# A new hand-written order of calls for the opening of a fused linear-attention and MLP kernel

## The chip, the cores and the metric

The kernel runs on one core of a Trainium2 chip. Its time is the device time of one execution in microseconds (us); several executions of the same program are timed, and their median counts. Beside them one execution is taken by the hardware profiler; it has a time of its own and a span, from its first instruction to its last. The engines are TensorE (PE in the profile, its weight loads PEld), VectorE (DVE), ScalarE (ACT), GpSimd (POOL) and SyncE (SP, which here only issues transfers).

## What is computed

Linear attention with a decay per head, in blocks, and behind it a two-layer MLP whose activation has a slope `alpha` for negative values. q, k and v are (4 batches, 8 heads, 768 positions, 64), the weights 512 x 2048 and 2048 x 512, all float32.

```python
for b in range(nb):                      # blocks of 64 positions
    intra = einsum('bhic,bhjc->bhij', qb, kb) * Dmask
    intra = einsum('bhij,bhjd->bhid', intra, vb)
    inter = einsum('bhid,bhde->bhie', qb * lam_pow, kv_state)
    out[:, :, sl] = intra + inter
    kv_state = lam_block * kv_state + einsum('bhsd,bhse->bhde', kb * rev_pow, vb)
x = out.transpose(0, 2, 1, 3).reshape(3072, 512)
h = x @ w_in
return (maximum(h, 0) + alpha * minimum(h, 0)) @ w_out
```

## The kernel before

The work is cut into six chunks (L41) of 512 tokens: chunk c holds 256 positions (block pair c // 2) of two batches (2 * (c % 2) and the next one, `bi` 0 and 1). Attention goes by units: unit n is a chunk, a `bi` and a half of the heads (`hh`), n = 4c + 2bi + hh (L240), so that chunk 0 is units 0 to 3 and chunk 1 units 4 to 7. The blocks used are of 128 positions, two in a unit.

What a unit needs, by the names in the code: `load` (L80) brings k, q or v of one chunk and `bi` as float32 through SP's queue, for all heads (`None`, 512 KB) or one half of them (256 KB). `cast` (L257) makes a half-precision copy of q, k or v of a unit on ScalarE ("A"), VectorE ("V") or GpSimd ("G"). `key_decayed` (L270) multiplies the raw k by its decay. `transposed` (L313) transposes q (x = 0) or k (x = 1) of a unit on TensorE, four products into a PSUM bank ("op", "tk" or "h"), and copies them out; `transposes` (L287) does both at once, or by a transfer ("D", from unit 9 on). `decayed` (L331) multiplies the transposed q by its decay, out of SBUF or, with "P", out of PSUM on VectorE. `cluster(old, new)` (L346) then does the products: for the unit `old` the part from the state (RD) and the part from masked scores and v, for the unit `new` its scores and the state's update; then VectorE's two mask products (L416), the copy of the result of `old` into XT (L423) and the states: for the first block pair two RD copies and an R copy on ScalarE (L436, L437) and two R updates on VectorE (L440), later R updates and four copies on GpSimd (L454). The accumulator `acc` (L350) has one buffer, so one cluster's products wait until the copies of the one before have read it.

The MLP of a chunk: `up(c, f)` (L459) is one of 16 groups of columns of w_in, four products over 512 tokens or, with `bi`, over 256; ScalarE takes relu(-h) (L472), VectorE makes g (L481). `down(c, t, part, 4)` (L488) is a quarter of the sum for 128 output rows. The weights come in quarters, cast on the way, by GpSimd's queue (`load_win`, `load_wout`); up(c, f) needs quarter f // 4 of w_in, and part p of a down-product quarter p of w_out. `gate` (L109) puts a tiny transfer that reads a weight quarter into SP's queue, so that all loads behind it wait until that quarter is there.

The decay tables are made by ScalarE and VectorE in the opening: `mask_logs` (L193) on VectorE, which reads `rel_f` in the bank "op"; `decay_mask`, `key_decay`, `state_decay` and `query_decay` (L206 to L229) on ScalarE. `fill(n)` (L133) issues n products of 128x512 whose result nothing reads ("unread" in the profile).

The schedule is by hand (L30): every engine and queue takes its instructions in the order in which the calls stand, and waits where its data or its buffer isn't ready. From L565 to L866 this order is a flat list of calls, the opening: the set-up, all of chunk 0 and 1, and the start of chunk 2; behind it a loop (L868) weaves the rest by a fixed pattern. In the list before, unit 0 to 3's clusters stand at L608, L618, L625, L634, L637 and L643, the unread products at L571, L575, L609, L623 and L627, the first up-product at L641, the first down-product at L677. SP's loads of chunk 0 start with both halves of k of `bi` 0, then q, then v; the two gates are at L633 and L670.

Of the kernel before, what the change touches and what calls it, by code (L numbers as in the profile page):

```python
# [11 lines left out]
def kernel(  # L12
# [24 lines left out]
    B, H, S, D = q.shape  # L37
# [418 lines left out]
    G = {}  # L456
# [105 lines left out]
                a[i]()  # L562
                i += 1

    query_decay(2, 0)  # L565
    query_decay(2, 1)
    load(0, 0, "k", 1)
    load(0, 0, "k", 0)
    load(0, 0, "q", None)
    query_decay(1, 1)  # L570
    fill(11, "h")  # L571
    load(0, 0, "v", 0)
    mask_logs(0)
    mask_logs(2)
    fill(6, "h")  # L575
    load(0, 0, "v", 1)
    key_decay()
    key_decayed(0, "G")
    mask_logs(3)
    load(0, 1, "k", 0)  # L580
    cast(1, "k16", "G")
    cast(0, "v16", "G")
    decay_mask(0)
    cast(0, "k16", "V")
    mask_logs(1)
    cast(2, "k16", "G")
    key_decayed(1, "G")
    load_win(0)
    load(0, 1, "q", None)
    cast(0, "q16", "V")  # L590
    state_decay()
    transposed(0, 1, "V", "op")
    load(0, 1, "k", 1)
    decay_mask(2)
    transposed(0, 0, "V", "h")
    transposed(1, 1, "V", "op")
    query_decay(0, 1)
    load(0, 1, "v", None)
    decay_mask(1)
    key_decayed(2, "G")  # L600
    load(1, 0, "k", 0)
    decay_mask(3)
    load_win(1)
    query_decay(3, 1)
    decayed(0, "P")
    cast(1, "q16", "A")
    load_win(2)
    cluster(None, 0)  # L608
    fill(5, "h")  # L609
    transposed(1, 0, "A", "h")  # L610
    cast(1, "v16", "A")
    cast(3, "q16", "G")
    transposed(2, 1, "V", "h")
    decayed(1, "P")
    load_win(3)
    cast(2, "q16", "V")
    load_wout(2)
    cluster(0, 1, "A")  # L618
    transposed(2, 0, "A", "tk")
    cast(2, "v16", "V")  # L620
    decayed(2, "V")
    cast(4, "k16", "V")
    fill(8, "h")  # L623
    load(1, 0, "q", 0)
    cluster(1, 2, "A")  # L625
    cast(3, "k16", "A")
    fill(5, "op")  # L627
    cast(3, "v16", "G")
    cast(4, "q16", "G")
    transposed(3, 0, "V", "tk")  # L630
    key_decayed(3, "V")
    transposed(3, 1, "A", "h")
    gate(2, "out")  # L633
    cluster(2, None, "A")  # L634
    load(1, 1, "k", 1)
    key_decayed(4, "G")
    cluster(None, 3, "A")  # L637
    decayed(3, "G")
    slopes()
    transposes(4, "A", False)  # L640
    up(0, 1, 0, "h")  # L641
    up(0, 3, 0, "op")
    cluster(3, None, "A")  # L643
    up(0, 2, 0, "h")
    load(1, 0, "v", 0)
    up(0, 2, 1, "h")
    decayed(4, "V")
    load(1, 0, "q", 1)
    load_wout(0)
    up(0, 0, None, "op")  # L650
    up(0, 7, None, "tk")
    up(0, 5, None, "h")
    load_wout(1)
    up(0, 6, None, "op")
    up(0, 10, None, "tk")
    up(0, 11, None, "h")
    zero_states((2,), "G")
    up(0, 14, None, "h")
    load(1, 0, "k", 1)
    load(1, 1, "q", 1)  # L660
    query_decay(3, 0)
    up(0, 13, None, "tk")
    up(0, 15, None, "op")
    up(0, 4, 1, "h")
    up(0, 4, 0, "h")
    load(1, 0, "v", 1)
    load(1, 1, "v", 1)
    up(0, 9, None, "tk")
    load(1, 1, "q", 0)
    gate(1, "out")  # L670
    up(0, 12, None, "op")
    up(0, 3, 1, "h")
    up(0, 8, None, "h")
    query_decay(0, 0)
    up(0, 1, 1, "tk")
    load(1, 1, "k", 0)
    down(0, 0, 0, 4, "op")  # L677
    down(0, 2, 0, 4, "h")
    down(0, 2, 1, 4, "h")
    key_decayed(7, "G")  # L680
    load_wout(3)
    load(1, 1, "v", 0)
    zero_states((3,), "V")
    load(2, 0, "k", 0)
    cast(4, "v16", "G")
    key_decayed(5, "G")
    cast(7, "q16", "A")
    load(2, 0, "q", 0)
    down(0, 3, 0, 4, "h")
    cast(6, "k16", "G")  # L690
    cast(5, "q16", "V")
    cast(5, "k16", "V")
    down(0, 3, 1, 4, "h")
    cluster(None, 4)
    transposes(5, "A", False)
    load(2, 0, "v", 0)
    cast(6, "v16", "G")
    load(2, 0, "q", 1)
    cast(5, "v16", "A")
    cast(7, "v16", "V")  # L700
    down(0, 0, 1, 4, "op")
    decayed(5, "V")
    load(2, 1, "k", 0)
    cast(7, "k16", "A")
    cast(8, "q16", "G")
    down(0, 2, 2, 4, "h")
    query_decay(1, 0)
    load(2, 0, "k", 1)
    cluster(4, 5, "A")
    transposes(7, "A", False)  # L710
    load(3, 1, "q", 0)
    key_decayed(8, "G")
    decayed(7, "P")
    down(0, 0, 2, 4, "op")
    cast(6, "q16", "A")
    down(0, 3, 2, 4, "h")
    cluster(5, 7, "A")
    down(0, 0, 3, 4, "op")
    cast(10, "k16", "G")
    load(2, 1, "k", 1)  # L720
    load(2, 1, "q", None)
    load(2, 0, "v", 1)
    key_decayed(6, "V")
    transposes(6, "A", False)
    load(3, 0, "v", None)
    down(0, 2, 3, 4, "h")
    load(2, 1, "v", None)
    down(0, 3, 3, 4, "h")
    decayed(6, "P")
    cast(8, "k16", "V")  # L730
    cluster(7, 6, "A")
    transposes(8, "A", False)
    down(0, 1, 0, 4, "h")
    cast(8, "v16", "V")
    cast(9, "k16", "G")
    cast(10, "q16", "G")
    down(0, 1, 1, 4, "h")
    cluster(6, 8, "A")
    load(4, 0, "q", 1)
    key_decayed(10, "G")  # L740
    down(0, 1, 2, 4, "h")
    up(1, 4, None, "op")
    key_decayed(11, "G")
    up(1, 1, None, "tk")
    cast(9, "q16", "V")
    transposes(9, "D", False)
    decayed(8, "G")
    load(3, 0, "k", None)
    down(0, 1, 3, 4, "h")
    up(1, 7, None, "op")  # L750
    cast(10, "v16", "G")
    transposes(10, "D", False)
    up(1, 13, None, "tk")
    up(1, 5, None, "h")
    up(1, 12, None, "op")
    cast(11, "k16", "G")
    load(3, 1, "k", 0)
    key_decayed(9, "G")
    cast(9, "v16", "V")
    up(1, 11, None, "h")  # L760
    up(1, 0, None, "h")
    cast(12, "k16", "G")
    up(1, 3, None, "op")
    up(1, 2, None, "tk")
    up(1, 8, None, "h")
    up(1, 9, None, "op")
    load(3, 0, "q", 1)
    load(3, 0, "q", 0)
    up(1, 6, None, "h")
    decayed(9, "G")  # L770
    cast(11, "q16", "A")
    cluster(None, 9)
    up(1, 15, None, "h")
    cast(12, "q16", "G")
    down(1, 0, 0, 4, "tk")
    up(1, 10, None, "h")
    key_decayed(13, "V")
    decayed(10, "V")
    down(1, 1, 0, 4, "op")
    down(1, 0, 1, 4, "tk")  # L780
    load(4, 0, "k", None)
    cast(11, "v16", "G")
    transposes(11, "D", False)
    cluster(8, 10, "A")
    cast(14, "k16", "A")
    cast(14, "q16", "V")
    transposes(12, "D", False)
    load(3, 1, "v", None)
    load(4, 0, "q", 0)
    down(1, 1, 1, 4, "op")  # L790
    load(3, 1, "k", 1)
    down(1, 1, 2, 4, "op")
    key_decayed(12, "V")
    decayed(11, "V")
    up(1, 14, None, "h")
    down(1, 2, 0, 4, "h")
    cluster(9, None, "A")
    down(1, 2, 1, 4, "h")
    cast(13, "q16", "A")
    cast(13, "k16", "V")  # L800
    cluster(10, 11, "V")
    decayed(12, "V")
    down(1, 2, 2, 4, "h")
    load(4, 1, "v", None)
    cast(14, "v16", "A")
    key_decayed(14, "G")
    down(1, 0, 2, 4, "tk")
    load(3, 1, "q", 1)
    cast(12, "v16", "A")
    transposes(13, "D", False)  # L810
    down(1, 1, 3, 4, "op")
    cast(13, "v16", "A")
    down(1, 0, 3, 4, "tk")
    key_decayed(16, "G")
    cluster(11, 12, "A")
    down(1, 2, 3, 4, "h")
    up(2, 9, None, "op")
    up(2, 4, None, "h")
    up(2, 0, None, "h")
    cast(15, "q16", "V")  # L820
    cast(16, "k16", "G")
    up(2, 5, None, "op")
    up(2, 3, None, "h")
    cast(15, "k16", "V")
    decayed(13, "G")
    up(2, 7, None, "h")
    transposes(14, "D", False)
    cluster(12, 13, "A")
    load(4, 1, "q", None)
    decayed(14, "G")  # L830
    load(4, 0, "v", None)
    key_decayed(17, "V")
    key_decayed(15, "G")
    transposes(15, "D", False)
    load(4, 1, "k", None)
    up(2, 8, None, "op")
    cast(18, "q16", "G")
    cast(16, "q16", "G")
    up(2, 1, None, "tk")
    down(1, 3, 0, 4, "h")  # L840
    down(1, 3, 1, 4, "h")
    cluster(13, 14, "V")
    down(1, 3, 2, 4, "h")
    cast(15, "v16", "V")
    down(1, 3, 3, 4, "h")
    cast(17, "k16", "G")
    up(2, 2, None, "tk")
    up(2, 11, None, "h")
    up(2, 10, None, "h")
    decayed(15, "G")  # L850
    transposes(16, "D", False)
    cluster(14, 15, "A")
    up(2, 14, None, "tk")
    cast(16, "v16", "A")
    cast(17, "q16", "A")
    up(2, 6, None, "h")
    decayed(16, "G")
    up(2, 13, None, "op")
    up(2, 15, None, "h")
    transposes(17, "D", False)  # L860
    cast(18, "k16", "G")
    cluster(15, 16, "A")
    cast(17, "v16", "G")
    up(2, 12, None, "tk")
    cast(18, "v16", "G")
    key_decayed(18, "G")  # L866

    for c in range(3, NC):  # L868
        att = []
# [39 lines left out]
```

## Time and profile before

| | |
|---|---|
| median of 3 runs (lowest, highest) | 216.26 us (216.04, 216.28) |
| the profiled execution, its time | 217.79 us |
| its span | 216.0 us |
| mean granted TensorE clock | 0.992 |
| TensorE busy | 207.9 us, 96% of the span |
| VectorE, ScalarE, GpSimd busy | 138.2, 114.3, 85.5 us |
| unread products in the opening (L140) | 35, 10.3 us |
| read from, written to memory | 27.27 MB, 6.29 MB |

Times inside the span are read from the profile's timeline, which gives start, length and instruction; its chain in order of time is the work that ended last, followed back from the last instruction; its windows give each engine's busy time in a stretch, and the clock that TensorE was granted there. An instruction's length holds the time in which it was held up after it began.

### The profile page before, as it was taken

The numbers are of one execution on the slowest core, as the hardware profiler recorded it, in microseconds if no ns is written. First come the engines' busy times: TensorE is split into PE (matmuls) and PEld (weight loads), VectorE is DVE, ScalarE is ACT, GpSimd is POOL, SyncE is SP. The second block draws the span as 40 slices with busy tenths as digits, with TensorE's granted clock in tenths as the row PEclk, the third lists the DMA queues.
The fourth block names the chain that finished last, engine by engine and source line by source line (L and its number), as shares of the span: only waits on it lengthen the run. The fifth ranks groups of instructions, "written<-read, shape, count | busy, mean of one in ns | idle before, by whom it ended". The sixth has DMA issues, their size and how long they took to land.

```text
span 216.0 us, 5257 instructions
## 1 busy us (share of the span) xinstructions
PE 207.9 (96%) x2097; PEld 107.7 (50%) x2097; DVE 138.2 (64%) x274; ACT 114.3 (53%) x218; POOL 85.5 (40%) x153
## 2 busy tenths in 40 slices
PE   7868999999999999999999999999999999999993
PEld 2534645556544555455554554554555444444462
DVE  7996788578688997898975745655647344444000
ACT  6854777398567354644845545554534543444121
POOL 3597404234196546549677367357311000000000
PEclk9988999999999999999999999999999999999999
DMA  6999999997999999994493977043011001110212
GB/s 179 292 268 207 205 206 299 226 302 219 297 219 234 285 245 217 205 279 121 36 246 93 208 199 194 6 100 97 3 49 49 35 16 49 50 49 3 99 63 83
DMA packets 61596, 33.64 MB, mean 156 GB/s; under 512 B 17268, under 2 KB 58628, under 8 KB 61572
## 3 DMA queue, kind: packets, MB, share of 16 engines
q1 hardware_dynamic: 57300, 29.10, 54.8%
q0 software_dynamic: 4224, 4.19, 11.8%
q8 instruction: 16, 0.26, 0.5%
q14 instruction: 8, 0.07, 0.1%
q10 hardware_dynamic: 48, 0.01, 0.0%
HBM read 27.27 MB, written 6.29 MB: 155 GB/s over the span
## 4 chain that ended last, share of the span: by engine, by line
PE 91%; DMA 3%; DVE 2%; ACT 1%; issue 1%; SPq 0%; ACTq 0%; DVEq 0%
PE h_ps L464 39%; PE o_ps L494 33%; PE o_ps L517 6%; PE s L378 4%; DMA qraw<-in_q_dram 3%; PE acc L390 2%; PE acc L361 2%; PE unread L140 1%; PE acc L405 1%; DVE qk L246 1%; PE tp L302 1%; PE tpx L322 1%; SPq L87 0%; DVE qkT L246 0%; DVE sm L416 0%
## 5 line engine op out<-in xcount | busy, mean ns | idle before, releaser
L481 DVE SCALAR_TENSOR_TENSOR g<-m,oma,h_ps 128x512 f16<-128x512 f32 (+1 forms) x100 | 71.6, 724 | 49.0 <-ACT m L472 46.3
L464 PE MATMUL h_ps<-xT,w_in_sb 128*128 128x512 f16 (+1 forms) x400 | 92.8, 371 | 0.0
L472 ACT ACTIVATE m<-h_ps 128x512 f32<-128x512 f32 (+1 forms) x100 | 57.5, 580 | 55.0 <-PE h_ps L464 53.3
L494 PE MATMUL o_ps<-w_out_sb,g 128*128 128x512 f16 x320 | 79.8, 379 | 0.0
L464 PEld LDWEIGHTS <-w_in_sb 128*128 128x128 f16 x400 | 38.5, 98 | 42.8
L494 PEld LDWEIGHTS <-g 128*128 128x128 f16 x320 | 30.1, 98 | 34.1
L454 POOL COPY RD<-R 64x128 f16<-64x128 f16 x64 | 21.3, 333 | 42.2 <-DVE R L440 40.4
L416 DVE TENSOR_TENSOR sm<-s,dmask 128x512 f16<-128x512 f32 x48 | 30.8, 682 | 7.2 <-PE s L378 7.0
L274 POOL TENSOR_TENSOR kdec<-kraw,kdecay 128x512 f16<-128x512 f32 x19 | 19.8, 1048 | 15.5 <-DMA kraw<-in_k_dram 11.7
L507 ACT ACTIVATE o_sb<-o_ps 128x512 f32<-128x512 f32 (+2 forms) x26 | 14.6, 565 | 21.2 <-PE o_ps L517 10.9
L244 ACT ACTIVATE xT<-acc 128x512 f16<-128x512 f32 x22 | 13.2, 598 | 13.7 <-PE acc L405 12.0
L336 POOL TENSOR_TENSOR qdT<-qkT,qdecay 128x512 f16<-128x512 f16 (+1 forms) x14 | 16.1, 1148 | 1.8 <-DVE qkT L246 1.6
L440 DVE SCALAR_TENSOR_TENSOR R<-R,rdecay,acc 128x64 f16<-128x64 f16 x64 | 14.2, 272 | 1.9 <-ACT R L437 1.8
L517 PE MATMUL o_ps<-w_out_sb,g 128*128 128x512 f16 (+2 forms) x96 | 14.1, 308 | 0.0
L248 POOL CAST qk<-kraw 128x512 f16<-128x512 f32 x15 | 9.6, 637 | 11.2 <-DMA kraw<-in_k_dram 10.5
L517 PEld LDWEIGHTS <-g 128*128 128x128 f16 x96 | 8.1, 98 | 6.1
L378 PE MATMUL s<-qkT 64*64 64x128 f16 x384 | 10.0, 222 | 0.4 <-ACT qkT L244 0.2
L140 PE MATMUL unread<-ident 128*128 128x512 f16 x35 | 10.3, 448 | 0.0
L390 PE MATMUL acc<-sm,v 64*64 64x128 f16 x384 | 9.6, 217 | 0.0
L361 PEld LDWEIGHTS <-RD 128*128 128x128 f16 x80 | 6.4, 99 | 5.8 <-issue 1.6
L361 PE MATMUL acc<-qdT,RD 128*128 128x128 f16 x80 | 8.5, 221 | 0.2 <-DVE R L440 0.2
L248 POOL CAST v<-vraw 128x512 f16<-128x512 f32 x13 | 8.4, 650 | 0.7 <-DMA vraw<-in_v_dram 0.7
(62 smaller groups left out, 118.6 us busy)
## 6 DMA issues: line engine op xcount, KB each, us to landing
out_dram<-o_sb SPq DMA_DIRECT2D x23, 256.0 KB, 2.3
vraw<-in_v_dram SPq DMA_DIRECT2D x8, 512.0 KB, 6.1
kraw<-in_k_dram SPq DMA_DIRECT2D x14, 256.0 KB, 6.4
qraw<-in_q_dram SPq DMA_DIRECT2D x6, 512.0 KB, 6.0
qraw<-in_q_dram SPq DMA_DIRECT2D x12, 256.0 KB, 6.1
kraw<-in_k_dram SPq DMA_DIRECT2D x5, 512.0 KB, 5.7
vraw<-in_v_dram SPq DMA_DIRECT2D x8, 256.0 KB, 5.7
w_in_sb<-in_moe_w_in_dram POOLq DMA_DIRECT2D x4, 512.0 KB, 9.0
```

The costliest lines, as they stand in the source:

```text
L248: nc.gpsimd.tensor_copy(out=out, in_=in_)
L274: engine(eng).tensor_tensor(out=kdec, in0=kr, in1=kdecay[:, ds(4 * hh, 4), :].rearrange("p h e -> p e h").unsqueeze(3).to_broadcast([128, ...
L336: engine(eng).tensor_tensor(out=qdT[:, :, :, p], in0=(t["qps"] if eng == "P" else t["qkT"][:, 0])[:, :, :, p], in1=qdecay[:, hh, :, :, p], ...
L361: nc.tensor.matmul(ot[a][:, hp, :].rearrange("p (e j) -> p e j", e=2), lhsT=RD[bb, ho][:, a, hp].rearrange("p h d -> p (h d)"), rhs=to["qd ...
L378: nc.tensor.matmul(s[hl][ds(a * 64, 64), hp, 1 - e, :].rearrange("p (e j) -> p e j", e=2), lhsT=t["qkT"][p, 1, e, hp, ds(a * 64, 64)], rhs ...
L416: nc.vector.tensor_tensor(out=sm, in0=s[hl], in1=mask_of(hl, hh), op=ALU.mult)
L454: nc.gpsimd.tensor_copy(out=RD[b, hh][p, a, :, hl, :], in_=R[b, hh, 2 * pb + a][p])
L464: nc.tensor.matmul(h_ps[:, 0:n] if bi is None else h_ps[:, 0:n].rearrange("p (e j) -> p e j", e=2), lhsT=w_in_sb[:, gi, ts(f, 128)], rhs=x ...
L472: nc.scalar.activation(m[:, 0:n], h_ps[:, 0:n], AF.Relu, scale=-1.0)
L481: nc.vector.scalar_tensor_tensor(out=g, in0=mv, scalar=oma[:, f : f + 1], in1=hv, op0=ALU.mult, op1=ALU.add)
L494: nc.tensor.matmul(o_ps, lhsT=lhs(c, f, t), rhs=w_out_sb[:, f, :], start=(f == 0), stop=(f == NF - 1),)
L517: nc.tensor.matmul(o_ps[:, 0:n], lhsT=lhs(c, f, t), rhs=w_out_sb[:, f, ds(x, n)], start=(f == 0), stop=(f == NF - 1),)
```

## The change

Only the list of calls of the opening is written anew; no function changes, and the loop behind it stays. All that the list did before it does again, in another order, with these differences:

- Casts, copies and small products go to other engines. Over the list VectorE has 12 casts (17 before), GpSimd 30 (25), ScalarE 15 (15); key decays are 8 on VectorE and 11 on GpSimd (5 and 14), decayed q 7 and 10 (10 and 7).
- 29 unread products in nine groups of 2 to 5 stand where 35 in groups of 5 to 11 stood; none of them is ahead of unit 1's first transposes.
- Chunk 0's loads: q of `bi` 0 first and whole, then half 0 of k, v whole, half 1 of k; of `bi` 1 half 0 of q, then k and v whole, then the other half of q.
- w_in's quarters are asked for in the order 3, 1, 0, 2 (0, 1, 2, 3 before), w_out's in the order 2, 0, 1, 3 as before. The second gate is on a quarter of w_in and stands between chunk 2's loads.
- The up-products of chunk 0 start at group 12. Three groups of the opening are cut into halves (four before).
- Chunk 1's units go through the clusters in the order 4, 5, 7, 6 as before.

The new list down to the cluster of units 6 and 8: its lines that are new (+) or were kept in place; the removed ones are those of the old list, above.

```diff
@@ -562,308 +562,309 @@
...
+    key_decay()
+    mask_logs(3)
+    mask_logs(1)
+    load(0, 0, "q", None)
+    cast(0, "q16", "G")
+    cast(1, "q16", "A")
+    mask_logs(0)
+    zero_states((2,), "G")
+    load(0, 0, "k", 0)
+    query_decay(0, 1)
+    load(0, 0, "v", None)
+    load(0, 0, "k", 1)
+    query_decay(3, 1)
+    transposed(1, 0, "A", "tk")
+    state_decay()
     query_decay(2, 1)
+    decay_mask(1)
+    cast(0, "k16", "G")
+    load(0, 1, "q", 0)
+    mask_logs(2)
+    fill(4, "h")
+    key_decayed(0, "V")
+    transposed(0, 0, "V", "op")
+    load(0, 1, "k", None)
     query_decay(1, 1)
+    cast(0, "v16", "G")
+    load(0, 1, "v", None)
+    transposed(0, 1, "V", "tk")
+    decayed(0, "V")
+    decay_mask(0)
+    fill(4, "h")
+    cast(1, "v16", "G")
+    cluster(None, 0)
+    decayed(1, "V")
     cast(1, "k16", "G")
+    decay_mask(3)
+    cast(2, "q16", "G")
+    fill(5, "tk")
+    decay_mask(2)
     key_decayed(1, "G")
+    transposed(1, 1, "A", "h")
+    cluster(0, None, "A")
+    load(0, 1, "q", 1)
+    load_win(3)
+    load(1, 0, "k", 0)
+    transposed(2, 0, "V", "op")
+    cast(2, "k16", "A")
+    cluster(None, 1, "A")
+    fill(3, "tk")
+    cast(3, "k16", "V")
+    load(1, 0, "q", 0)
+    transposed(2, 1, "A", "op")
+    fill(3, "h")
+    slopes()
+    cast(2, "v16", "A")
+    key_decayed(3, "V")
+    key_decayed(2, "G")
+    load_win(1)
     load_win(0)
+    cast(3, "q16", "V")
+    query_decay(1, 0)
     load_win(2)
+    cluster(1, 2, "A")
+    decayed(2, "G")
+    cast(3, "v16", "V")
+    cast(4, "k16", "V")
+    load_wout(2)
+    fill(3, "tk")
+    cast(4, "q16", "V")
+    transposed(3, 0, "A", "op")
+    transposed(3, 1, "A", "tk")
+    fill(2, "h")
+    decayed(3, "P")
+    gate(2, "out")
+    cluster(2, 3, "A")
+    transposes(4, "V", False)
+    key_decayed(4, "G")
     fill(5, "h")
+    up(0, 12, 0, "h")
+    cluster(3, None, "A")
+    decayed(4, "V")
+    load_wout(0)
+    load_wout(1)
+    up(0, 14, 0, "h")
+    up(0, 15, None, "tk")
+    up(0, 14, 1, "h")
+    load(1, 0, "q", 1)
+    load(1, 0, "v", 0)
+    cast(5, "q16", "G")
+    load(1, 0, "k", 1)
+    up(0, 13, None, "op")
+    up(0, 5, None, "h")
+    load_wout(3)
     load(1, 1, "k", 1)
+    zero_states((3,), "G")
+    up(0, 4, None, "h")
+    up(0, 6, None, "tk")
+    up(0, 12, 1, "op")
+    up(0, 2, None, "h")
+    up(0, 7, None, "h")
+    up(0, 10, None, "op")
+    up(0, 11, None, "h")
+    up(0, 1, None, "tk")
+    up(0, 3, None, "h")
+    load(1, 0, "v", 1)
     up(0, 0, None, "op")
     load(1, 1, "q", 1)
+    up(0, 8, None, "h")
+    up(0, 9, None, "tk")
+    cast(5, "k16", "G")
+    cast(4, "v16", "V")
+    down(0, 3, 0, 4, "h")
+    down(0, 2, 0, 4, "h")
+    load(1, 1, "v", 1)
+    key_decayed(5, "G")
+    cast(5, "v16", "G")
+    down(0, 0, 0, 4, "op")
+    cluster(None, 4)
+    load(1, 1, "k", 0)
+    load(1, 1, "q", 0)
+    down(0, 0, 1, 4, "op")
+    transposes(5, "V", False)
+    cast(7, "v16", "G")
+    load(1, 1, "v", 0)
+    cast(7, "k16", "A")
+    down(0, 3, 1, 4, "h")
+    cast(7, "q16", "V")
+    load(2, 0, "k", None)
+    down(0, 2, 1, 4, "h")
+    transposes(7, "V", False)
+    key_decayed(7, "V")
+    cluster(4, 5, "A")
+    load(2, 0, "q", 0)
+    down(0, 2, 2, 4, "h")
+    gate(3, "in")
+    cast(6, "k16", "A")
+    load(2, 0, "v", None)
+    down(0, 3, 2, 4, "h")
+    cast(6, "q16", "V")
+    decayed(5, "G")
+    load(4, 0, "k", 1)
+    down(0, 0, 2, 4, "op")
+    cluster(5, 7, "A")
+    load(2, 1, "k", 0)
+    down(0, 0, 3, 4, "op")
+    load(2, 0, "q", 1)
+    transposes(6, "A", False)
+    key_decayed(6, "V")
     query_decay(3, 0)
     decayed(6, "P")
     cast(8, "k16", "V")
+    load(2, 1, "q", None)
+    cast(6, "v16", "G")
+    query_decay(2, 0)
+    decayed(7, "G")
+    cast(8, "q16", "V")
+    cast(8, "v16", "G")
+    down(0, 3, 3, 4, "h")
+    cast(9, "q16", "G")
+    down(0, 1, 0, 4, "op")
     cluster(7, 6, "A")
+    query_decay(0, 0)
+    load(2, 1, "v", None)
+    down(0, 1, 1, 4, "op")
     transposes(8, "A", False)
+    down(0, 2, 3, 4, "h")
+    cast(10, "q16", "G")
+    load(3, 0, "q", None)
+    key_decayed(8, "V")
+    up(1, 13, 0, "h")
+    load(3, 0, "k", None)
     cast(9, "k16", "G")
+    transposes(9, "D", False)
     cluster(6, 8, "A")
...
```

## The prediction

> **What bounds the kernel now.** I read the page's slices first, then the chain in order of time, then TensorE's windows and the timeline of the opening. The slices and windows say that TensorE is busy for all of 36 to 212 us (176.00 of 176.00) and for 31.58 of the first 36. A list that changes only the order can win time only ahead of the dense stretch, and lose it anywhere. The chain in order of time, from the middle of the opening on (start, length, what):
>
> ```profile
> 12.15 1.87 DVE qk L246
> 14.06 0.40 PE tpx L322 x4
> 14.46 3.23 PE unread L140 x8
> ...
> 24.40 0.35 PE acc L390 x16
> 24.75 13.22 PE h_ps L464 x72
> 37.97 0.22 PE o_ps L494
> ```
>
> The reader is to see two long pieces that do no needed work: a cast of VectorE, 1.87 us, and eight unread products, 3.23 us. Behind the sum-up of unit 3 (24.40) the up-products run without a gap until the first down-product at 37.97. The timeline around the cast (start, length, instruction):
>
> ```profile
> 11.71 0.93 POOL L96 DMA_DIRECT2D w_in_sb<-in_moe_w_in_dram  x1
> 12.06 1.95 DVE L246 CAST qk<-qraw 128x512 f16<-128x512 f32 x1
> 12.65 1.06 POOL L274 TENSOR_TENSOR kdec<-kraw,kdecay 128x512 f16<-128x512 f32 x1
> ```
>
> The same cast costs 0.42 where GpSimd is idle. Here it ends 0.3 behind GpSimd's key decay: 1.53 us of waiting for the other engine. TensorE idles 1.49 us for it, and then its granted clock falls (windows of 1 us; the column behind POOL's is the clock):
>
> ```profile
> 14.00:15.00 1.00, 0.94 (x7) 0.54 (x8) 1.00 (x3) 0.50 (x1) 1.00 (x2) 0.76 1.24 266
> 15.00:16.00 1.00, 1.00 (x4) 0.37 (x3) 1.00 (x4) 0.10 (x1) 1.00 (x3) 0.50 1.21 211
> 17.00:18.00 1.00, 1.00 (x12) 0.46 (x14) 0.00 (x0) 0.00 (x0) 1.00 (x3) 0.53 1.24 207
> 18.00:19.00 1.00, 1.00 (x51) 0.72 (x44) 0.67 (x2) 0.31 (x1) 1.00 (x2) 1.00 1.22 204
> ```
>
> At clock 0.50 one unread product takes 0.43 us instead of 0.216; so eight cost 1.5 us more than at full clock.
>
> **The change, part by part.** I walk the new list by hand, each engine in its order, with the durations of the opening's rows: cast 0.62 on GpSimd and ScalarE, 0.42 on VectorE; key decay 1.05 on GpSimd, 0.68 on VectorE; four transposes 0.25 to 0.40, their copy 0.60 on ScalarE, 0.42 on VectorE; mask product of a unit 1.29; RD,RD,R 0.85 on ScalarE; R 0.46; xT 0.60; scores 0.40; a weight DMA's issue 0.77.
>
> Loads. DMA moves about 290 KB per us from 3 us on in either order, so the n-th 256 KB should land when the n-th did (issue plus time to landing: 1st 3.8, 2nd 4.8, 4th 7.2, 7th 10.0, 10th 12.8, 12th 14.6). That estimate gives q of batch 0 at 4.8, its k half 0 at 6.0, v at 8.1, k half 1 at 9.1; of batch 1 q half 0 at 10.0, k at 12.0, v at 13.7, q half 1 at 14.6. The latter was whole at 12 before; it is needed late. The ten chunk-0 and chunk-1 loads up to the gate are the same bytes, and GpSimd reaches the first weight load at 11.7 as before (six casts, two memsets and one key decay, the last from 10.65, with waits for the loads between them), so the weights land from 19 us on as before; the first up-product needs its quarter at 22.
>
> Unit 0. ScalarE: key decay to 5.28, cast of q for unit 1 to 5.9. TensorE idles from 3.3 to 5.95 (seventeen unread products covered this before), then transposes, four products at half clock (6.2 to 7.9), eight transposes to 8.4, four more products to 10.1. VectorE's copies end at 9.2. Scores of unit 0 start at **10.1**, before 9.11: the list loses 1.0 here. Mask product 10.55 to 11.84.
>
> Unit 1. ScalarE is the path: RD,RD,R to 11.6, two masks to 12.6, copy of unit 1's k to 13.2. Scores at 13.25 (11.74 before), mask product 13.65 to 14.94 (before 13.93 to 15.20, since it stood behind the stalled cast). The lists are level. xT 13.8, cast 14.42, RD,RD,R 15.27, copy 15.87.
>
> Unit 2. Scores at **16.0** against 17.84: no stalled cast, and six unread products at 0.216 where eight took 3.23. VectorE now holds R (15.73), cast 0.42, oma 0.17, key decay 0.68, cast 0.42, together to 17.4; mask product 17.4 to 18.7 (before 18.33 to 19.62).
>
> Unit 3. R to 19.15, scores 19.6 (21.67). VectorE: v, k and q casts 1.25 to 20.4, decayed q to 20.8, mask product 20.8 to 22.1 (22.13 to 23.42), R to 22.56. Cluster (3, none) 22.6 to 23.1, xT to 23.7; the first full up-product at **23.75**. Two half products lie ahead of it; the remaining 14 full and two half take 12.99, so the down-products start at 36.74 against 37.97: **-1.2 us**.
>
> The six unread products that go stood in waits: nothing. Of those that stay, 16 stand behind 14 us at 0.216 each, inside waits for ScalarE and VectorE; without that cover they cost 3.5. The later half gives TensorE the same up, down and cluster products, 48 and 32 and 17; moved casts (VectorE 17 to 12, GpSimd 25 to 30, ScalarE 15 to 15) lie under a full TensorE: nothing, as long as each comes in time. SP loses its second gate, so chunk 1's loads follow the first gate unbroken; the last weight load on GpSimd stands behind one cast and is issued at about 36.3 (36.55 before), needed at 48.5.
>
> Meetings. In my walk VectorE's key decay of unit 3 (16.3) meets GpSimd's decayed q of unit 2 (15.95 to 16.95), and decayed q of unit 0 meets casts at 9.2. Rows for two-input work beside GpSimd:
>
> ```profile
> 73.73 0.79 DVE L274 TENSOR_TENSOR kdec<-kraw,kdecay 128x512 f16<-128x512 f32 x1
> 74.44 1.09 DVE L336 TENSOR_TENSOR qdT<-qkT,qdecay 128x512 f16<-128x512 f16 x1
> ```
>
> Alone these take 0.68 each: a meeting costs 0.11 to 0.41, with 1.53 (the stalled cast) as upper end and 0 as lower. I take **0.3**, near the two rows of the same operations, since only the meeting at 16.3 is on the path. The Trainium skill, "SBUF — State Buffer", Who interferes with whom, says that whoever starts second is blocked for the whole of the other's instruction; by it the key decay would wait 0.65 and the sum would be -0.55. The row of 0.79, begun 0.24 before a GpSimd cast ended, shows 0.11, less than such a block.
>
> Sum: -1.2 + 0.3 = **-0.9 us**. The profiled execution took 217.79, its span 216.0; so 216.9 and a span of 215.1. Its time is 1.53 above the median of the runs, 216.26; from that median -0.9 is **215.4**.
>
> **Rivals.**
>
> 1. *Better still.* If the first eight unread products run at full clock and nothing meets, unit 0's scores come at 8.9 and the walk gains another 1.4 to the end: -1.2 - 1.4 = -2.6, 213.7. For it: before, full clock came at 4.4 after 3.2 us of products. Against: the new list leaves TensorE idle from 3.3 to 5.95. Chance 0.15.
>
> 2. *Half clock comes back: slower.* Place: the fall of the clock at 14.7 us again, or one at 18 to 21. Price: unread products after 14.7 at 0.43 delay units 2 and 3 by 0.6; if the half clock of 3.3 us (14.75 to 18.05 in the rows) lies over the first up-products instead, half of it is lost: 1.65, so 217.05; both, 217.65. It decides from about 2.6 us of up-products at half clock. For it: six unread products fewer and a wait of 2.65 early. Against: in my walk TensorE is busy about 85% of every 3.4 us from 7.8 on; before, the stretch ahead of the fall (11.24 to 14.65) was busy about 50%, and 80% elsewhere kept the clock. The Trainium skill, "TensorE: Matmul & The Clock Gate", What's actually happening, says that the clock is halved by default and raised after about 3.4 us of sustained activity; the 4.4 and the 3.3 of the rows agree, and by it the new list starts units 0 and 1 at half clock, as I have walked. Chance 0.14.
>
> 3. *Dense stretch breaks.* Between 39.6 and 47.5 VectorE now has two units' 1024-wide copies (0.82 each, an estimate from two of 0.42; ScalarE took 1.02 before) beside two mask products, two R, a cast and a key decay: 6.3 us, and R of unit 5 ends at 46.9 where cluster (5, 7) wants the one acc bank at 47.5. A stall like 12.06's (1.53) there leaves TensorE idle 0.9; two such places give -0.9 + 1.8 = +0.9, 217.2. For it: every gap costs its full length, as no slack is left behind it. Against: no gap before in 176 us. Chance 0.16.
>
> 4. *The casts meet anyway.* The title's aim fails: one meeting at 1.53 instead of 0.3, or the walk's VectorE chain (15.3 to 22.6 with hardly a gap) is late by 0.9: 216.3, no change. For it: the old list's 1.53 is not to be read from its order. Chance 0.13.
>
> **How the numbers follow.** The forecast, 214.4 to 215.8, has 0.42. Faster by over 0.2% (0.43 us, about what a measurement of this kernel can tell from no change): 0.42 + 0.15 = 0.57. Within: 0.13. Slower: 0.14 + 0.16 = 0.30. For 8 in 10 I reach down to 213.9 (most of rival 1) and up to 217.3 (rival 3 and part of rival 2).
>
> **What would show it.** In the changed profile: the first down-product at about 36.7; unit 0's scores at 10 and unit 2's at 16; no VectorE cast above 0.6 before 24 us; the granted clock at 1.00 from about 11 on; TensorE busy all of 36 to 210. Wrong would be: clock 0.50 anywhere in 15 to 27, a gap of TensorE after 24, or scores of unit 3 after 21.

## The result and the profile after

The median of the changed kernel is **216.87 us** (eight executions, 216.73 to 217.55), that of the kernel before 216.22 (eight, 215.63 to 216.29): a ratio of 1.0042, interval 1.0028 to 1.0055, slower by 0.65 us. The profiled execution took 216.88 with a span of 215.1, at a mean granted clock of 1.0: the very numbers that the walk gave for a profiled execution, before 1.53 was taken off. An execution's time lies 1.7 to 1.9 above its span in both lists, and the two profiled ones lie 1.79 and 1.78 above theirs. Two executions far out, 308.1 us (the one that e0_before_again's profile took) and 430.2, are left out of everything below.

The chain of waits of the changed kernel (start, length, what), with the two groups of four unread products in unit 0, the long cast, and the end of the opening:

```profile
6.49 1.71 PE unread L140 x4
...
9.05 1.70 PE unread L140 x4
10.74 0.35 PE s L378 x16
...
17.24 1.28 DVE qk L246
...
23.90 13.50 PE h_ps L464 x68
37.40 2.59 PE o_ps L494 x12
```

The first down-product comes at 37.40 instead of 37.97. The piece of eight products (3.23) is gone; two pieces of four (3.41 together) stand ahead of unit 0's scores instead, and a cast of 1.28 is still there. The windows of the changed kernel (busy time of PE, PEld, DVE, ACT, POOL, then the clock):

```profile
4.00:6.00 2.00, 0.12 (x2) 0.12 (x3) 2.00 (x7) 1.99 (x5) 0.90 (x3) 1.00 1.16 303
6.00:8.00 2.00, 2.00 (x9) 0.90 (x9) 1.32 (x3) 1.88 (x7) 0.93 (x3) 1.00 1.16 290
14.00:16.00 2.00, 1.98 (x42) 1.14 (x42) 1.99 (x5) 1.86 (x6) 2.00 (x4) 1.00 1.22 252
16.00:18.00 2.00, 2.00 (x56) 1.11 (x54) 2.00 (x5) 1.63 (x5) 1.98 (x3) 1.00 1.23 208
24.00:205.00 181.00, 181.00 (x1747) 91.68 (x1746) 118.05 (x216) 94.50 (x173) 71.69 (x130) 1.00 0.64 151
```

Three things are to be seen. TensorE is idle from 4 to 6. Where the profiled execution of before had a clock of 0.50, the column now says 1.00. And from 24 to 205 TensorE has no gap, so what is lost is lost ahead of 24.

So the profiled execution got faster by 0.91 (217.79 to 216.88) while the median got slower by 0.65. The likeliest reading is that the profiled execution of before was an unusual one. Three theories were put to the test. *Theory 1*: the fall of the clock from 14.75 to 18.05, which I read as part of the old list, occurs in few of its executions; the usual one is 1.5 us faster than the page, and the new list loses against it since TensorE goes idle and starts unit 0 at half clock. *Theory 2*: the fall belongs to every execution of the old list, and the time beside the span differs between the lists. *Theory 3*, of the loss: the meeting at 17.24 is what it consists of.

### The profile page after: what moved, and what is told of

Read it like the earlier page. It is cut to its first block, busy times and chain, and to the rows that moved or that the text cites. A ratio compares the mean times of both kernels' runs of the same rounds, so it can differ in the third digit from the quotient of the medians.

```text
span 215.1 us, 5246 instructions
## 1 busy us (share of the span) xinstructions
PE 206.4 (96%) x2087; PEld 106.5 (50%) x2087; DVE 137.5 (64%) x267; ACT 112.3 (52%) x216; POOL 87.0 (40%) x160
## 3 DMA queue, kind: packets, MB, share of 16 engines
q0 software_dynamic: 4224, 4.19, 11.8%
## 4 chain that ended last, share of the span: by engine, by line
PE 93%; DVE 2%; ACT 2%; issue 1%; ACTq 0%
PE h_ps L464 39%; PE o_ps L494 33%; PE o_ps L517 6%; PE s L378 4%; PE acc L390 3%; PE acc L361 2%; PE unread L140 2%; PE acc L405 1%; PE tp L302 1%; PE tpx L322 1%; PE unread L138 1%; DVE qk L246 1%; DVE sm L416 1%; ACT L213 1%; ACT dmask L207 0%
## 5 line engine op out<-in xcount | busy, mean ns | idle before, releaser
L454 POOL COPY RD<-R 64x128 f16<-64x128 f16 x64 | 19.7, 308 | 39.4 <-DVE R L440 37.6
L507 ACT ACTIVATE o_sb<-o_ps 128x512 f32<-128x512 f32 (+2 forms) x26 | 14.7, 565 | 19.6 <-PE o_ps L517 10.9
L336 POOL TENSOR_TENSOR qdT<-qkT,qdecay 128x512 f16<-128x512 f16 (+1 forms) x17 | 18.7, 1099 | 1.5 <-DVE qkT L246 1.0
L274 POOL TENSOR_TENSOR kdec<-kraw,kdecay 128x512 f16<-128x512 f32 x16 | 16.9, 1059 | 0.1
L248 POOL CAST qk<-qraw 128x512 f16<-128x512 f32 x11 | 7.1, 648 | 23.8 <-DMA qraw<-in_q_dram 23.6
L248 POOL CAST v<-vraw 128x512 f16<-128x512 f32 x15 | 9.2, 615 | 8.7 <-DMA vraw<-in_v_dram 5.1
L248 POOL CAST qk<-kraw 128x512 f16<-128x512 f32 x14 | 9.0, 646 | 3.1 <-DMA kraw<-in_k_dram 2.7
L140 PE MATMUL unread<-ident 128*128 128x512 f16 x29 | 9.4, 450 | 0.0
```

The source lines that it names most:

```text
L248: nc.gpsimd.tensor_copy(out=out, in_=in_)
L274: engine(eng).tensor_tensor(out=kdec, in0=kr, in1=kdecay[:, ds(4 * hh, 4), :].rearrange("p h e -> p e h").unsqueeze(3).to_broadcast([128, ...
L336: engine(eng).tensor_tensor(out=qdT[:, :, :, p], in0=(t["qps"] if eng == "P" else t["qkT"][:, 0])[:, :, :, p], in1=qdecay[:, hh, :, :, p], ...
L454: nc.gpsimd.tensor_copy(out=RD[b, hh][p, a, :, hl, :], in_=R[b, hh, 2 * pb + a][p])
```

## The experiments

Each edit is against the kernel named. A ratio is to the kernel before, measured beside the run, with its 95% interval. Where I say "usual", executions with a mean granted clock under 0.994 are left out; the number of executions stands in brackets.

**The kernel before again**, unchanged, with a profile (two runs: e0_before_again, e4_before_third).

> The kernel before, unchanged, with span and granted clock of every execution. Theory 1: its profiled execution (217.79 us, span 216.0, clock 0.992) was not a usual one. The fall of the clock from 14.75 to 18.05 happens in few executions and costs about 1.5 us where it does (eight unread products at 0.43 us instead of 0.216, plus what follows). Then most executions show a clock of 1.00, a span of 214.2 to 214.7 and a time of 216.0 to 216.4, and a profile of such a one has its first down-product at about 36.4 instead of 37.97. Theory 2: the profiled execution is like all others and only its time outside the span is longer; then the span is 216.0 and the clock 0.992 in every execution, and the difference to the changed kernel is made by something that its profile doesn't show.

> The kernel before, unchanged, for a profile of a usual execution. Theory 1 by the granted clocks so far (35 executions: 30 at a clock of 0.997 to 1.00, median 216.2 us; 5 at 0.990 to 0.992, 217.9 to 219.1): most likely a clock of 1.00 and a span of 214.4. The eight unread products behind the transposes of unit 2 then take 1.7 us instead of 3.4, scores of unit 2 come at 16.3 instead of 17.84 and the first down-product at 36.4 instead of 37.97. If the span is near 214.4 and the down-product still at 37.9, theory 1 has the wrong place.

Measured: with the runs of before that stand beside the other kernels, 139 executions. (The kernel before against itself, 11 executions against 35, gave a ratio of 1.0026, 0.999 to 1.0062, with medians 0.5 us apart: so much can come from nothing.) 18 have a clock of 0.990 to 0.992, and these took 217.75 to 219.12, median 218.1; the other 121 have a median of 216.36. No execution of before has a clock between 0.992 and 0.996 (a few of the others took 217.0 to 218.2 at a clock of 0.996 or more): the fall costs 1.7 us and happens in about one execution of eight. The profiled execution of before (217.79, clock 0.992) is of the kind of the 18. The one profiled as e4_before_third (216.12, span 214.3) is usual. Its windows over the eight products, and its chain:

```profile
13.00:14.00 1.00, 0.33 (x5) 0.34 (x6) 1.00 (x2) 0.67 (x3) 1.00 (x2) 1.00 1.17 289
14.00:15.00 1.00, 1.00 (x8) 0.41 (x6) 1.00 (x4) 0.60 (x1) 1.00 (x3) 1.00 1.27 291
15.00:16.00 1.00, 1.00 (x18) 0.54 (x20) 1.00 (x4) 0.00 (x0) 1.00 (x2) 1.00 1.16 200
```

```profile
9.75 0.61 POOL qk L248
10.36 1.01 POOL kdec L274
11.37 0.87 POOL w_in_sb L96
12.26 1.06 POOL kdec L274
...
22.71 13.23 PE h_ps L464 x72
35.94 4.32 PE o_ps L494 x20
```

The stalled cast is there as before (11.77, 1.84), and TensorE waits for it (0.33 busy), but the clock stays at 1.00: the eight products start at 13.90 and are through in 1.89, unit 2's scores come at 15.83 where the page had 17.84, and the first down-product at 35.94 where it had 37.97. The first half of theory 1 holds (the fall is not part of every execution), and theory 2 has fallen. The chain of this execution leads through GpSimd and not through TensorE, so the eight products aren't even on the path here.

**The early products.** They are put into the changed list (e1_early_products, and again as e9_early_products_again):

```diff
     mask_logs(1)
+    fill(11, "h")
     load(0, 0, "q", None)
```

and the reverse in the list before, without its seventeen (e10_before_without_early), with the changed list unaltered beside it (e8_changed_again):

```diff
-    fill(11, "h")
...
-    fill(6, "h")
```

> The changed kernel with eleven unread products put at the head of the list. Theory 1 with its second half (the changed list loses its time because TensorE stands idle from 3.3 to 5.9 us and then runs the two groups of four unread products ahead of unit 0's scores at half clock, 3.4 us on the path): the eleven products raise the clock at about 4.4, the two groups take 0.9 us each, unit 0's scores come at 8.8 instead of 10.7, and of these 1.9 us about 1.4 reach the end, since VectorE's chain takes up the rest: a span of 213.7, a time of 215.5. Rival theory 3 (VectorE's chain and the loads set units 1 to 3 whatever unit 0 does): unit 0 comes earlier, the end stays within 0.3 us of the changed kernel, 216.9. Rival theory 4 (more products cost time): slower than 217.0.

> The changed kernel with eleven unread products at the head of the list, a second time, now beside the changed kernel itself. Theory 1 (half clock in unit 0 is what the changed list loses): faster than the changed kernel by 0.8 to 1.4 us, 215.5 to 216.1, and faster than the kernel before by 0.3 us or more. If the gain of the first time was the chip's, it falls together with the changed kernel within 0.3 us.

> The kernel before without its seventeen unread products ahead of unit 0, the counterpart. Theory 1 in its plain form (an early raise of the clock is worth 0.8 us or more in any list of this opening): slower by about 0.8, 217.1, with the five products behind unit 0 at 0.43 us. Theory 3 (here unit 2 waits for VectorE's cast and GpSimd until 13.7 to 14.0 whatever units 0 and 1 do): within 0.3 us of 216.3 in the usual executions, the lost 1.0 us taken up by TensorE's wait at 12.6.

> The changed kernel, unchanged, beside the kernel before and the next one on the same chip. Theory 1: executions with no fall of the clock at 216.7 to 217.0, the kernel before at 216.2 to 216.4 in its usual executions and at about 218 in one of six. So 0.3% slower where both are undisturbed, and no execution of the changed kernel at a clock below 0.995.

Measured: e1 216.07, ratio 0.9964 (0.9926 to 1.0002), usual 215.66 (10); e9 216.39, ratio 0.9993 (0.9962 to 1.0024), usual 215.92 (9), against 216.84 of the changed list beside it (e8, ratio 1.0026, 1.0012 to 1.0039). The old list without the products: 216.90, ratio 1.0028 (1.0006 to 1.0049), usual 216.88 against 216.25, slower by 0.63. So taking them away costs the old list as much as the change cost, and giving them back to the new one gains 0.9 to 1.2 between the medians of usual executions, or 0.45 to 0.8 with all executions counted. TensorE's instructions of the changed kernel and of e1 (start, length, operation):

```profile
6.28 1.91 PE L140 MATMUL unread<-ident 128*128 128x512 f16 x4
7.99 1.06 PE L322 MATMUL tpx<-ident,qk 128*128 128x128 f16 x8
8.84 1.90 PE L140 MATMUL unread<-ident 128*128 128x512 f16 x4
10.68 0.42 PE L378 MATMUL s<-qkT 64*64 64x128 f16 x16
```

```profile
3.21 3.16 PE L140 MATMUL unread<-ident 128*128 128x512 f16 x11
6.43 1.03 PE L140 MATMUL unread<-ident 128*128 128x512 f16 x4
7.74 1.03 PE L140 MATMUL unread<-ident 128*128 128x512 f16 x4
8.70 0.42 PE L378 MATMUL s<-qkT 64*64 64x128 f16 x16
```

Four products take 1.91 without the eleven and 1.03 with them (both lengths hold some 0.2 of pipeline); unit 0's scores come at 8.70 and not 10.68. But the profiles of e8 and e9 show that this is only half of the account (starts of the scores and of the first down-product):

| profiled execution | unit 0's scores | unit 3's scores | first down-product | span | time |
|---|---|---|---|---|---|
| before, usual (e4) | 8.77 | 19.64 | 35.94 | 214.3 | 216.12 |
| changed | 10.68 | 20.44 | 37.40 | 215.1 | 216.88 |
| changed again (e8) | 9.65 | 20.39 | 37.35 | 215.1 | 216.84 |
| early products (e1) | 8.70 | 17.84 | 35.55 | 213.7 | 215.53 |
| early products again (e9) | 9.73 | 20.29 | 37.25 | 214.9 | 216.76 |

In e8 the changed list itself starts unit 0 a whole us earlier, since its second group of four already runs at full clock (1.03), and it gains 0.05 at the first down-product. In e9 the same eleven products take 4.19 instead of 3.16, as the clock is raised later, and they gain next to nothing. VectorE takes up the difference. In e8 its decayed q of unit 1, 0.42 alone, meets GpSimd's key decay and ends 0.30 behind it:

```profile
11.77 1.91 DVE L336 TENSOR_TENSOR qdT<-qkT,qdecay 128x256 f16<-128x256 f16 x1
12.32 1.06 POOL L274 TENSOR_TENSOR kdec<-kraw,kdecay 128x512 f16<-128x512 f32 x1
```

In e1 the same instruction begins at 10.81 and is through at 11.72, before that key decay begins, and the cast of q of unit 3 begins at 15.20 instead of 17.24 and takes 0.66. So an early unit 0 pays where it brings VectorE past these meetings: all of 1.85 us at the first down-product in e1, next to none for the first us. The 24 executions of e1 and e9 lie in three heaps: 214.7 to 216.3 (13), 216.7 to 216.9 (6, the time of the changed list), and 218.2 to 218.5 (5, the low clock, which the changed list itself showed in none of 19). The profiles of e1 and e9 are of the first and of the second heap; that the moment of the raise divides the two is likely, and not shown for the others.

In the old list without its seventeen (e10) the loss has another place than in the changed list: unit 0's scores still come at 8.77, but the five products behind them take 2.32 instead of 1.25, unit 1's scores come at 12.98 instead of 11.54, and the first down-product at 37.14.

**The changed list without the eight products of unit 0** (e2_without_eight): both `fill(4, "h")` are taken out. (The 29 unread products of the new list stand in eight groups, not nine.)

> The changed kernel without the two groups of four unread products ahead of unit 0's scores, so that TensorE is at half clock but has nothing unneeded to do there. If the products themselves are what holds unit 0 (theory 1): scores of unit 0 at 8.4, and about 1.4 us less at the end, 215.5, unless the clock now stays at half for longer, which then shows at the later unread products and the first up-products and costs up to 1.7 us: 217. If VectorE's chain sets units 1 to 3 (theory 3): within 0.3 us of 216.9, or slower by the clock alone.

Measured: 216.07 (12), ratio 0.9971 (0.9942 to 1.0), 0.8 below the changed list. The products were a loss where they stood: unit 0's scores come at 8.26. By TensorE's timeline the long run of up-products starts at 22.49 instead of 23.83, but a gap of 0.37 us opens at 38 to 40: unit 4's products wait for VectorE's cast of v, 1.84 long beside GpSimd. I tried to close it by giving that cast to ScalarE (e7_without_eight_v4_scalar, e2 with `cast(4, "v16", "A")`); the gap of 1.4 us in that expectation is a misreading of mine.

> The changed kernel without the two groups of four unread products, and with the cast of v of unit 4 on ScalarE instead of VectorE. Without the eight alone, the profile had TensorE dense from 22.5 us on (23.8 in the changed kernel), but lost 1.4 us at 38 to 39.4, where the products of k and v of unit 4 waited for this cast, 1.84 us on VectorE behind three operations of GpSimd. Theory 1 (the eight products cost about 1.3 us in the opening, and the meeting gave it back): TensorE has no gap behind 24 us, and the time is 214.8 to 215.3 against 216.1 without the eight alone. Rival: the gap stays, as v of unit 4 lands late; then 216.0.

Measured: 217.12, ratio 1.0017 (0.9981 to 1.0053), in three heaps: 215.7 to 215.9 (4), 217.0 to 217.2 (5), 218.5 (3, clock 0.989 to 0.992). In the profiled one, of the middle heap, five products at 9.06 take 2.32, and 2.11 in e2: the clock is raised later. Nothing follows for the cast. That the moment of the raise makes the heaps is likely, and not shown.

**The meeting at 17.24.** The changed kernel's timeline:

```profile
16.64 0.68 DVE L274 TENSOR_TENSOR kdec<-kraw,kdecay 128x512 f16<-128x512 f32 x1
16.96 1.26 POOL L274 TENSOR_TENSOR kdec<-kraw,kdecay 128x512 f16<-128x512 f32 x1
17.24 1.27 DVE L246 CAST qk<-qraw 128x512 f16<-128x512 f32 x1
```

The cast, 0.41 alone, ends 0.29 behind GpSimd's key decay of unit 4. In e3_no_meeting this decay is moved behind the next weight load:

```diff
-    key_decayed(4, "G")
...
     load_wout(1)
+    key_decayed(4, "G")
```

> The changed kernel with the key decay of unit 4 on GpSimd moved behind the second weight load of w_out, so that it no longer meets VectorE's cast of q of unit 3, which took 1.27 us at 17.24 instead of 0.42. If that meeting lies on the path (theory 1 takes it for 0.85 us of the loss, theory 3 for all of it): the cast ends at 17.65, the mask product of unit 2 begins 0.8 earlier, and the time falls by 0.8 to 216.1. If unit 3 is held by TensorE or by ScalarE instead: within 0.2 us of 216.9, with a wait for something else in the cast's place.

Measured: 216.64, ratio 1.0008 (0.9976 to 1.0041); 0.2 below the changed list's 216.84, where 0.8 was expected. The cast of q now takes 0.41, but the one before it stalls:

```profile
15.62 0.71 POOL L336 TENSOR_TENSOR qdT<-qkT,qdecay 128x256 f16<-128x256 f16 x1
15.84 1.43 DVE L246 CAST qk<-kraw 128x512 f16<-128x512 f32 x1
```

The meeting moves to another instruction, so this edit doesn't decide theory 3; giving the cast to a third engine, below, says more. With the early products as well (e11_early_and_late_decay, e1's edit and e3's):

> The changed kernel with eleven early unread products and with the key decay of unit 4 behind the second weight load of w_out. With the early products VectorE's cast of v of unit 3 took 1.15 us at 17.35 beside that decay. If the meeting goes and no other takes its place: 0.5 us less than with the early products alone, 215.0 to 215.4. If meetings only move, as with the decay moved in the changed kernel (another cast took 1.43) : within 0.3 us of it.

Measured: 216.33 (12), ratio 0.9974 (0.9946 to 1.0002): the two gains don't add up in the usual case. The casts of q and v of unit 3 take 1.58 and 1.15 in the profiled execution (216.31). Two of the twelve took 214.32 and 214.70, 1.5 below the rest, and were not profiled.

**In the list before: the eight products, and the stalled cast.** e5_before_four_ahead puts four of the eight into TensorE's wait, e6_before_cast_scalar gives the stalled cast to ScalarE:

```diff
+    fill(4, "h")
     transposed(2, 0, "A", "tk")
...
-    fill(8, "h")
+    fill(4, "h")
```

```diff
-    cast(2, "q16", "V")
+    cast(2, "q16", "A")
```

> The kernel before with four of those eight unread products put ahead of the transposes of q of unit 2, into the time in which TensorE waits for VectorE's stalled cast. Theory 1 (the fall of the clock needs that wait, and the products behind it are on the path): no execution at a clock below 0.995, and the usual one faster by four products at 0.216, 0.9 us: 215.3. If the fall comes from elsewhere, the share of executions at 0.992 stays at about one in six. If unit 2 is held by VectorE's queue rather than by the products, the median stays at 216.2.

> The kernel before with one cast dealt out anew and nothing else: the stalled cast of q of unit 2 goes from VectorE to ScalarE. If the meeting with GpSimd is what the old list lost, the one thing that the change is named for: the cast ends at 12.9 instead of 14.0, TensorE's wait and the fall of the clock go, scores of unit 2 come at about 15.2, and the time falls by about 1.0 to 215.2. If VectorE's next operation waits for GpSimd in its place, or ScalarE's copies come later by the 0.6 us added, within 0.3 us of 216.2.

Measured: e5 216.52, ratio 1.0 (0.9968 to 1.0033), two of 12 at the low clock: no gain, which fits the usual chain through GpSimd. (Its profile is of an execution of 218.68 at a clock of 0.999, and is not read here.) e6 216.14, ratio 0.998 (0.9949 to 1.0011), usual 216.12 (11) against 216.40: -0.3 where -1.0 was expected. In its profile, of an execution at the low clock, unit 2's scores come at 15.0, but now VectorE's key decay of unit 3 stalls:

```profile
18.68 2.02 DVE L274 TENSOR_TENSOR kdec<-kraw,kdecay 128x512 f16<-128x512 f32 x1
```

**Both of VectorE's troubles at once.** The cast at 17.24 on ScalarE, alone (e12_changed_cast_scalar), with e2's edit (e13_without_eight_cast_scalar) and with e1's (e14_early_cast_scalar):

```diff
-    cast(3, "q16", "V")
+    cast(3, "q16", "A")
```

> The changed kernel with the cast of q of unit 3 on ScalarE, the one that took VectorE 1.27 us at 17.24 beside GpSimd's key decay. If that meeting is on the path and does not move (the key decay moved away in an earlier run only shifted it to another cast, 0.2 us): VectorE's chain to unit 3 loses 1.27, ScalarE's gains 0.5, scores of unit 3 at about 19.6 instead of 20.4, 216.0 against 216.85. If meetings move, the next cast of VectorE takes the wait: within 0.3 us of 216.85.

> The changed kernel without the two groups of four unread products and with that cast on ScalarE. The two causes add up if each holds the path by itself: 0.8 from the products and 0.8 from the cast, 215.2. If they don't (with unit 0 earlier, the loads or GpSimd's order set unit 3), within 0.3 us of the 216.1 without the eight alone.

> The changed kernel with eleven early unread products and with that cast on ScalarE. As before: 0.9 and 0.8, 215.0 in the usual executions if the two add up, 215.7 to 215.9 if they don't. Executions with a fall of the clock (218.2 to 218.5, five of 24 with the early products alone) stay as frequent if the fall has nothing to do with VectorE's cast, and go if TensorE's wait for that cast is where it begins.

Measured: e12 216.49, ratio 0.9995 (0.997 to 1.002); e13 216.45, ratio 0.9991 (0.9965 to 1.0017); **e14 215.98, ratio 0.9966 (0.9937 to 0.9994)**, faster than the kernel before. None of these 36 executions has the low clock.

What the cast costs is seen between executions in which unit 0 starts at the same time. In e12's profile its scores come at 9.75, as in e8's (9.65); unit 3's come at 19.03 instead of 20.39, and the long run of up-products at 22.50 instead of 23.85. In e14's they come at 9.64, as in e9's (9.73); the first down-product comes at 36.05 instead of 37.25. So the cast on VectorE costs the opening 1.2 to 1.35 us: it takes 1.26 there, some 0.85 by the meeting and 0.41 by its own length. The second half of theory 1 and theory 3 are each right in part. The opening becomes shorter by more than 1 us with the cast away from VectorE (e12), or with unit 0 two us earlier (e1, e2), and neither alone is the whole loss.

The times show less of it than the spans. In e12, e13 and e14, and in e7, an execution takes 2.1 to 2.2 us more than its span, in all other kernels 1.7 to 1.9 (the kernel before, beside them, 1.7 to 1.9 as well); no run says why. The median spans are 215.1 for the changed list, 214.35 for e12, 214.3 for e2 and for e13, and 213.85 for e14. So e12 gains 0.75 inside its span, where 0.8 was expected of its time, and e13's time is above e2's (216.07) by what lies beside the span alone. In e13 the two edits don't add up.

In e12's profile part of the gain is given back behind the opening; VectorE's and GpSimd's rows there, and the window:

```profile
37.33 1.88 DVE L246 CAST v<-vraw 128x512 f16<-128x512 f32 x1
37.86 1.06 POOL L274 TENSOR_TENSOR kdec<-kraw,kdecay 128x512 f16<-128x512 f32 x1
```

```profile
38.00:40.00 2.00, 1.58 (x37) 0.80 (x36) 2.00 (x3) 0.21 (x1) 1.53 (x2) 1.00 1.19 246
```

TensorE is idle for 0.42: the cast of v stands beside GpSimd's cast and key decay and meets them when the opening ends early.

## Why the prediction was wrong

*The walk* was right to about 0.6 us. It gave unit 0's scores at 10.1, unit 2's at 16.0, unit 3's at 19.6 and the first down-product at 36.74; measured 10.68, 16.59, 20.44 and 37.40. The 0.6 arises in unit 0: the walk put the unread products at half clock (1.7 each, as measured) but the twelve transposes at full clock, 0.25 and 0.5, where the chain has 0.61 and 0.85. The first full up-product, walked at 23.75, comes at some 24.3, an estimate: a half product begins at 23.90 and takes 0.45, as the one at 22.84 does. With the 0.3 for meetings the walk gave 216.9 and a span of 215.1 for a profiled execution: 216.88 and 215.1. In part this is luck: the opening gained 0.57 (37.97 to 37.40) instead of 0.9, and the rest of the span is 0.33 shorter (178.03 to 177.70).

*The step that failed* is this: "Its time is 1.53 above the median of the runs, 216.26; from that median -0.9 is 215.4". The 1.53 isn't an offset that both lists carry. It comes from the fall of the clock, 1.7 us in 18 of 139 executions of the old list, and the profiled one was of their kind. What the new list was credited with (unit 2 at 16.0 "against 17.84", eight products that "took 3.23") was measured against this execution. Against a usual one the same walk says: first down-product 36.74 + 0.3 = 37.0 against 35.94, slower by 1.1. The two numbers stood beside each other in the prediction; windows at clock 0.50 and a time 1.53 above the median should have been read as one fact.

*"Seventeen unread products covered this before"*, and "the list loses 1.0 here": right, and too small against the usual execution (10.68 against 8.77 is 1.9; 0.9 in e8, where the clock was raised sooner). The walk let unit 2 make it good (16.0 against 17.84), and that holds against the profiled execution alone: in the usual one unit 2's scores come at 15.83. It is one of the two things that make the new opening longer than a usual old one, though by e8 and e9 the first us of it can be undone and the end hardly moves.

*Meetings*, "I take 0.3", and "only the meeting at 16.3 is on the path": the wrong place, and mis-sized. The key decay at 16.64 took its 0.68. The cast at 17.24 is 0.86 late (1.27 against 0.41), and without it on VectorE the opening is 1.2 to 1.35 shorter (e12 against e8, e14 against e9); "no VectorE cast above 0.6 before 24 us" was wrong. The page of the Trainium skill that I weighed, "SBUF — State Buffer", Who interferes with whom, was nearer: a blocked instruction waits until the other's is through, and the cast ended 0.29 behind the key decay.

*The rivals.* The first (better still) did not come, since the first eight products ran at half clock, as walked; in e8 the last four of them ran at full clock, and nothing came of it. The second (half clock comes back) didn't either: no low clock in 19 executions. The third: no gap in the dense stretch of the changed kernel; but a gap of 0.37 to 0.42 at unit 4 does come up when the opening is made shorter (e2, e12). The fourth (the casts meet anyway) is nearest to what happened; its 216.3 was too low since it, too, counts from the median with the 1.53 taken off.

*What stays open.* Of the 1.46 us by which the changed opening is later than a usual old one (37.40 against 35.94), 0.66 comes back, since from there on the changed execution is shorter (177.70 against 178.36). The old one has 0.19 of TensorE's idle time behind 64 us, and about 0.2 more from its last product to the end of the span (3.6 against 3.4); for the remaining 0.3 I have no row. Nor is it settled why a fall starts. It was seen behind a wait of 1.4 us for the stalled cast, but the same wait is there in the usual execution of before; e6's fall, without that cast, shows from 21 on (granted clock 0.80 in 21 to 22, 0.50 in 22 to 25), behind a wait of 1.41 us for VectorE's key decay. That e12 to e14 had none in 36, where the early products alone had five in 24, speaks for TensorE's wait at 17 to 18.5 as one place of its start; but the changed list has this wait too (1.07 in e8) and had none in 19, so it is not shown. Nor is it known what lies beside the span in e7 and e12 to e14.

## What to carry to other kernels

Before an opening is priced from one profile, compare the profiled execution's time, less what always lies beside the span, with the median: a difference of 1.5 us was an event on the page, to be found in the windows and taken out of the old kernel's side, not out of the new one's. Work that nothing reads can still be on the path both ways: in the old list, seventeen products in an idle stretch were worth 0.6; in the new one, eight ahead of unit 0's scores cost 0.8. An earlier start is worth nothing while a later wait takes it up (e8), so profile the same kernel a second time before a late start is called the loss. Moving GpSimd's instruction out of a meeting moved the meeting to another of VectorE's (0.2 us gained of 0.8); giving VectorE's instruction to ScalarE took it out of the opening (0.75 of the span). Look at the whole row of both engines before a meeting is given a price.

## What the runs showed of the hardware

The granted clock in the windows is 1.00 over the first products, though they take 0.43 each: the half clock of the start is seen only in the products' length. The raise comes at a varying time: eleven products from 3.28 on took 3.09 in the chain of e1 and 4.03 in that of e14. With n of them at 0.43 and the rest at 0.216, n is 3.3 and 7.7, so the raise came at 4.7 and at 6.6, or 3.5 and 5.4 us after TensorE's first product (1.19). The Trainium skill, "TensorE: Matmul & The Clock Gate", What's actually happening, speaks of about 3.4 us of activity; e1 agrees, e14 is later.

VectorE can be kept out for longer than one instruction of GpSimd. In e14 a product of two inputs that begins in the middle of a weight load's issue ends only behind the key decay that follows:

```profile
11.19 0.93 POOL L96 DMA_DIRECT2D w_in_sb<-in_moe_w_in_dram  x1
...
11.76 1.73 DVE L336 TENSOR_TENSOR qdT<-qkT,qdecay 128x256 f16<-128x256 f16 x1
...
12.13 1.06 POOL L274 TENSOR_TENSOR kdec<-kraw,kdecay 128x512 f16<-128x512 f32 x1
```

It ends at 13.49, 0.30 behind the key decay, though it needs 0.41 and began 0.37 ahead of it. In the usual execution of before a cast begun in such an issue (15.96, issue 15.34 to 16.09) took 0.42. Which of the two happens is not settled.
